# Head 0's preparation rebuilt: whole-row loads joined on SBUF, four reads of its turned tile, operands copied on SBUF

## The chip, the cores and the metric

The kernel runs on one core of one Trainium2 chip. The metric is the device time of one execution in microseconds, the median of several runs. TensorE, VectorE, ScalarE, GpSimd and SyncE (SP) each work through their own instructions strictly in order; DMAs are issued from SP's and GpSimd's queues.

## The reference, cut to what matters

Three stages follow one another. The first is attention with a bucket mask (2 batches, 8 heads, 768 positions, 64 channels); its output, 1536 tokens by 512, goes through two feed-forward stages.

```python
q_bits = (einsum('bhsd,dk->bhsk', q, proj) > 0);  k_bits = (einsum('bhsd,dk->bhsk', k, proj) > 0)   # 6 bits
mask   = q_bucket[:, :, :, None] == k_bucket[:, :, None, :]        # the bits as a number, 0 to 63
scores = where(mask, q @ k.T / sqrt(64), -1e9)
attn   = exp(scores - max) / (sum + 1e-9);   x = attn @ v          # then heads side by side
h = x @ w_in;  g = h * tanh(softplus(h));    x = g @ w_out         # d_ff 2048
out = ((x @ w1) * (x @ w2)) @ w3 @ w_out2                          # d_ff 1024
```

## The kernel before

The 16 heads (two batches of eight) are worked off one after another; head u has six row blocks of 128 queries. Each block has one score tile S of 128 x 768 in two PSUM banks (two halves of 384 columns), a maximum on VectorE (L619), an exponential on ScalarE (L622), six transposes of it (L666) and products with v (L695). Numbers are split into a rounded part and a remainder so that matmuls in a rounded format keep single precision: a score is the sum of two matmuls per half, one of the operands `kb`, `qb` (128 rows: rounded part and remainder of k and q) and one of `ka`, `qa` (76 rows: the rounded parts again, and 12 rows of mask).

`prep` (L485) makes these four operands for a head. `load_head` (L448) puts q and k of the head into one tile `rw`, so that each 128-position block holds q's 64 channels beside k's 64; every DMA piece is therefore 256 bytes. Six TensorE transposes (L514) turn it: PSUM tile with q's channels on partitions 0 to 63 and k's on 64 to 127. For heads 1 to 15 ScalarE writes the rounded part `hh` (L532) and VectorE the remainder (L534), each for all 128 partitions, and six DMAs (`move`, L480) put their halves where `qb`, `kb`, `qa`, `ka` want them; bucket bits come from matmuls with `psel2` on `hh` and the remainder (L565). For head 0 that way is not used: twelve reads of the turned tile of 64 x 384 each, six on ScalarE (L547) and six on VectorE (L550 to L557), write the operands directly, and the bits come from four matmuls per half on `qb` and `kb` with another selector, `psel`. A comparison (L576) then writes the mask rows into `qa`, and a copy (L443 for head 0, a DMA for the others) takes twelve of them to `ka`.

The turned tile and the bits tile lie, for head 0 and for heads from 3 on, in one two-bank score tile (`self.one`); heads 1 and 2 use two separate one-bank tiles. `HH` has two buffers, one head's `hh` and remainder; before, head 0 doesn't use it.

The order of all this isn't written by hand. `Plan.op` takes each step with its engine, an expected cost, an expected latency (`lat`), its reads and writes, and a due number; `Plan.run` is a list scheduler that gives every engine its order by these, and every engine's queue then holds that order. `after` only puts a step behind another's planned start. Between planned TensorE steps up to 60 us the plan fills gaps with zero matmuls (`zeros`, L427) that keep the engine running. At the start, `setup` (L1213) prepares constants: GpSimd sets tiles to zero, VectorE splits the projection into `pq` and fills `psel`, GpSimd fills `psel2` from `pq`. Behind it in GpSimd's queue stand sums over v (L465) and then the first weight loads (L754).

Of the kernel before, what the change touches and what calls it, by code (L numbers as in the profile page):

```python
# [320 lines left out]
def kernel(  # L321
# [14 lines left out]
    nc = tc.nc  # L336
# [73 lines left out]
    psel = ctile([128, 2, 2, 128], "psel", FR)  # L410
# [11 lines left out]
    v_id, v_psel, v_psel2, v_ccol, v_qks = Val(), Val(), Val(), Val(), Val()  # L422
# [25 lines left out]
    def load_head(u, due, after=()):  # L448
        b, h = divmod(u, H)
        t = raws[u] = Val(RW, "r")  # L450
        for x, (nm, src) in enumerate((("q", q), ("k", k))):
            P.op("SP", 0.5, lambda x=x, src=src: nc.sync.dma_start(
                out=t()[:, :, x], in_=src[b, h].rearrange("(p c) d -> p c d", c=C)), w=[(t, nm)], due=due,
                lat=None if u else 1.85, name=f"load{nm}{u}", after=after)

    def load_v(u, due, after=()):
        b, h = divmod(u, H)
        t = vs[u] = Val(VP, "v")
        P.op("SP", 0.5, lambda: nc.sync.dma_start(out=t(), in_=v[b, h].rearrange("(p c) d -> p c d", c=C)),
# [18 lines left out]
    def move(o, to, f, fr, r, w, due, name):  # L478

        P.op("SP", 0.5, lambda: nc.sync.dma_start(out=o()[to].bitcast(F32), in_=f()[fr].bitcast(F32)),  # L480
             r=r, w=w, due=due, lat=5.0, name=name)
# [3 lines left out]
    def prep(u, d0, step):  # L485
# [30 lines left out]
        hh, ll = (Val(HH, "h"), Val(HH, "l")) if u else (None, None)  # L516
        if u and t.one:
            P.op("PE", C * 0.118, tr, r=[raw], w=t.all() + [(hh, "t"), (ll, "t")], due=d(1), name=f"tq{u}", after=first_bits)
        else:
            for a in range(2):  # L520
                P.op("PE", CH * 0.118, lambda t=t, a=a: tr(t, range(a * CH, (a + 1) * CH)), r=[raw],
                     w=[t.key(a)] + ([(hh, "t"), (ll, "t")] if u and not a else []), due=d(1), name=f"tq{u}", after=first_bits if u else ())
        low, high = slice(0, D), slice(D, 2 * D)
        half = lambda v_: v_.rearrange("p (a n) -> p a n", a=2)
        if u:
            for x in ((slice(0, 2), ) if t.one else (slice(0, 1), slice(1, 2))):
                n = (x.stop - x.start) * HS
                cols = slice(x.start * HS, x.stop * HS)
                key = t.all()[x]
                src = (lambda t=t: t.v[0]()[:, :, 0:HS]) if t.one else (lambda t=t, x=x: t.at(x.start))  # L530
                dst = (lambda v_: half(v_())) if t.one else (lambda v_, cols=cols: v_()[:, cols])
                P.op("ACT", act(n) + 0.01, lambda src=src, dst=dst: nc.scalar.activation(  # L532
                    out=dst(hh), in_=src(), func=AF.Copy, scale=qks[:, 0:1]), r=key + [v_qks], w=[(hh, x.start)], due=d(1.3), name=f"hh{u}")
                P.op("DVE", dve(n), lambda src=src, dst=dst: nc.vector.scalar_tensor_tensor(  # L534
                    out=dst(ll), in0=src(), scalar=qks[:, 0:1], in1=dst(hh), op0=ALU.mult, op1=ALU.subtract),
                    r=key + [(hh, x.start), v_qks], w=[(ll, x.start)], due=d(1.6), name=f"ll{u}")
            for o, to, f, fr in ((qb, low, hh, low), (kb, high, hh, high), (qa, low, hh, low), (ka, low, hh, high),
                                 (qb, high, ll, low), (kb, low, ll, high)):
                move(o, to, f, fr, [f], [(o, to.start if o in (qb, kb) else "x")], d(2.2), f"fa{u}")
            ops = [(psel2[:, 0], hh), (psel2[:, 1], hh), (psel2[:, 0], ll)]  # L540
            needs = [hh, ll, v_psel2]
        else:
            inv = 1.0 / float(D) ** 0.5
            for a in range(2):
                cols = slice(a * HS, (a + 1) * HS)
                for o, p, fr, c in ((kb, high, high, inv), (ka, low, high, inv), (qb, low, low, 1.0)):
                    P.op("ACT", act(HS), lambda t=t, o=o, p=p, fr=fr, c=c, a=a, cols=cols: nc.scalar.activation(  # L547
                        out=o()[p, cols], in_=t.at(a)[fr], func=AF.Copy, scale=c), r=[t.key(a)],
                        w=[(o, ("x" if o is ka else p.start, a))], due=d(1.3 + 0.3 * a), name=f"hh{u}")
                P.op("DVE", dve(HS), lambda t=t, a=a, cols=cols: nc.vector.tensor_copy(out=qa()[low, cols], in_=t.at(a)[low]),  # L550
                     r=[t.key(a)], w=[(qa, ("x", a))], due=d(1.3 + 0.3 * a), name=f"hh{u}")
                P.op("DVE", dve(HS), lambda t=t, a=a, cols=cols: nc.vector.tensor_sub(
                    out=qb()[high, cols], in0=t.at(a)[low], in1=qa()[low, cols]), r=[t.key(a), (qa, ("x", a))],
                    w=[(qb, (D, a))], due=d(1.4 + 0.3 * a), name=f"ll{u}")
                P.op("DVE", dve(HS), lambda t=t, a=a, cols=cols: nc.vector.scalar_tensor_tensor(
                    out=kb()[low, cols], in0=t.at(a)[high], scalar=inv, in1=kb()[high, cols],
                    op0=ALU.mult, op1=ALU.subtract), r=[t.key(a), (kb, (D, a))], w=[(kb, (0, a))], due=d(1.5 + 0.3 * a), name=f"ll{u}")  # L557
            ops = [(psel[:, 0, 0], qb), (psel[:, 1, 0], kb), (psel[:, 0, 1], qb), (psel[:, 1, 1], kb)]
            needs = [qb, kb, v_psel]
# [7 lines left out]
        for a in range(2):  # L567
            r = needs if u else [(qb, (x, a)) for x in (0, D)] + [(kb, (x, a)) for x in (0, D)] + [v_psel]
# [18 lines left out]
        for a in range(2):  # L587
# [3 lines left out]
                 r=[(qa, ("m", a))], w=[(ka, ("m", a))], due=d(4.6), name=f"km{u}")  # L591

# [34 lines left out]
    def norm(u, due):  # L627
# [25 lines left out]
        P.op("SP", 0.5, lambda: nc.sync.dma_start(  # L653
# [161 lines left out]
    def wprod(f, d0, d1):  # L815
# [40 lines left out]
        P.op("SP", 0.5, lambda: nc.sync.dma_start(out=wp_d[f * 128:(f + 1) * 128], in_=o()[:, 0:DM]), r=[o], w=[(v_wp, f)],  # L856
# [9 lines left out]
    def x_split(n, due, after=()):  # L866
# [3 lines left out]
        for kk in range(KD):  # L870
# [5 lines left out]
            for e in range(2):  # L876
                P.op("SP", 0.5, lambda e=e, kk=kk, rb=rb: nc.sync.dma_start(
# [62 lines left out]
    def x_quarters(due, after=()):  # L940
        xs = []
        for i in range(2):
            xq_ = Quarters()
            xs.append(xq_)
            for n in (1, 2):
                t0, t1 = n * TB, (n + 1) * TB
                bs = range(t0 // S, (t1 - 1) // S + 1)
                for k1 in range(2):
# [5 lines left out]
                    for e in range(2):  # L954
                        P.op("SP", 0.5, lambda e=e, kk=kk, rb=rb, t0=t0, t1=t1: nc.sync.dma_start(
# [114 lines left out]
    def ff_first(n, d0, d1):  # L1070
# [107 lines left out]
        def o_group(G):  # L1178
# [3 lines left out]
            for t4 in range(TB // 128):  # L1182
# [15 lines left out]
                if G == GT // 2 - 1:  # L1198
                    P.op("SP", 0.5, lambda t4=t4, ov=ov: nc.sync.dma_start(out=rows_out(n, t4), in_=ov()), r=[(oacc, t4)],
                         due=dd(1.0), lat=3.0, name="out")  # L1200
# [12 lines left out]
    def setup():  # L1213
        pr = Val()
        for e in range(2):
            P.op("SP", 0.5, lambda e=e: nc.sync.dma_start(out=prow[e * D:(e + 1) * D], in_=proj), w=[(pr, e)], due=-10, lat=2.2, name="proj")
        cr, pz, p2z = Val(F4, "c"), Val(), Val()
# [9 lines left out]
        P.op("POOL", 0.5, lambda: nc.gpsimd.memset(psel.bitcast(F32), 0.0), w=[pz], due=-11, name="pz")  # L1227
        P.op("POOL", 0.8, crows, w=[cr], due=-10, name="crow")
        P.op("POOL", 0.2, lambda: nc.gpsimd.memset(psel2.bitcast(F32), 0.0), w=[p2z], due=-9, name="p2z")
# [18 lines left out]
        def pqs():  # L1248
            nc.vector.tensor_copy(out=pq[:, 0, 0], in_=prow)
# [293 lines left out]
```

## Time and profile before

| | |
|---|---|
| median of 3 runs | 781.59 us (781.08 to 782.19) |
| profiled execution | 781.81 us, its span 780.0 us |
| TensorE matmul / weight load | 765.0 us (98%) / 596.7 us (76%) of the span |
| VectorE / ScalarE / GpSimd | 557.8 us (72%) / 508.9 us (65%) / 105.4 us (14%) |
| DMA | 120.70 MB, of it 55.02 MB through SP's queue and 65.02 MB through GpSimd's |

Busy shares are means over the span. The chain that ended last is TensorE's for 91% of the span, with short pieces of VectorE (4%), ScalarE (2%) and DMA (1%); a matmul's end is modelled, so a TensorE shown busy is not one at its peak. A row's "idle before <- X" says how long the engine stood and what released it.

### The profile page before, as it was taken

The page shows a single profiled execution, that of the slowest core. Times are in us where ns is not written, and L with a number is a line of the kernel's source. Part 1 is how long each engine was busy: PE and PEld are TensorE (multiplying, and loading weights), DVE is VectorE, ACT ScalarE, POOL GpSimd, SP SyncE. Part 2 cuts the span into 40 slices and gives each one's busy share as a digit, 9 for nine tenths or more (in the row PEclk, how much of TensorE's full clock was granted, in tenths as well). Part 3 has the DMA queues.
Part 4 walks back from the last instruction along what each step waited for, and adds up shares of the span by engine and source line. Part 5 has one row for each costly group of instructions (what it writes and reads, how often), then busy time and mean ns, then how long its engine had stood idle before and what let it go on. Part 6 is the DMA issues. An engine that isn't in the chain of part 4 may idle for free.

```text
span 780.0 us, 10577 instructions
## 1 busy us (share of the span) xinstructions
PE 765.0 (98%) x3808; PEld 596.7 (76%) x3808; DVE 557.8 (72%) x812; ACT 508.9 (65%) x815; POOL 105.4 (14%) x204
## 2 busy tenths in 40 slices
PE   6999999999999999999999999999999999999998
PEld 5767888897577777777766888888888888788877
DVE  3897778889877986967996959764543848775620
ACT  3889667779799887868867835654544626443330
POOL 3222001222332222113212110000000000000000
PEclk8999999999999999999999999999999999999999
DMA  6997646697897768755465740431215310010011
GB/s 206 214 305 229 181 128 200 157 336 218 259 280 220 249 207 255 230 175 165 158 230 203 259 147 28 162 103 39 75 54 162 109 54 1 28 54 1 1 54 55
DMA packets 62252, 120.70 MB, mean 155 GB/s; under 512 B 29924, under 2 KB 32324, under 8 KB 61176
## 3 DMA queue, kind: packets, MB, share of 16 engines
q1 hardware_dynamic: 45944, 55.02, 25.4%
q0 software_dynamic: 16256, 65.02, 24.2%
q8 instruction: 30, 0.49, 0.3%
q14 instruction: 22, 0.18, 0.1%
HBM read 83.89 MB, written 17.87 MB: 130 GB/s over the span
## 4 chain that ended last, share of the span: by engine, by line
PE 91%; DVE 4%; ACT 2%; issue 1%; DMA 1%; SPq 0%; ACTq 0%; DVEq 0%
PE q L1005 20%; PE b L1419 11%; PE b L1065 9%; PE s L606 8%; PE b L695 8%; PE b L666 7%; PE b L1160 6%; PE b L1049 5%; PE b L846 5%; PE b L1461 5%; PE s L565 2%; PE s L514 1%; PE b L829 1%; DVE st L619 1%; DMA ka<-qa 1%
## 5 line engine op out<-in xcount | busy, mean ns | idle before, releaser
L1005 PE MATMUL q<-k,k 128*128 128x512 f32 x672 | 159.4, 395 | 0.0
L1005 PEld LDWEIGHTS q<-k,k 128*128 128x128 f32 x672 | 126.1, 188 | 30.4 <-DVE f L1020 0.4
L798 DVE TENSOR_TENSOR k<-f,k 128x1024 fp32r<-128x1024 f32 x92 | 111.7, 1220 | 20.5 <-ACT k L796 20.2
L796 ACT CAST k<-f 128x1024 fp32r<-128x1024 f32 x92 | 94.7, 1050 | 21.0 <-DVE f L988 6.4
L619 DVE TENSOR_REDUCE st<-s 128x1 f32<-128x768 f32 x96 | 90.9, 950 | 21.7 <-PE s L606 19.4
L622 ACT ACTIVATE E<-s,st 128x768 f32<-128x768 f32 x96 | 86.9, 905 | 25.1 <-DVE st L619 15.2
L666 PE MATMUL b<-ident,E 128*128 128x128 f32 x576 | 92.0, 274 | 0.2 <-DVE T L675 0.2
L1016 ACT COPY f<-q 128x512 f32<-128x512 f32 x64 | 37.5, 586 | 81.6 <-PE q L1005 78.6
L1020 DVE TENSOR_TENSOR f<-q,f 128x512 f32<-128x512 f32 x64 | 42.9, 686 | 65.8 <-PE q L1005 39.5
L1419 PE MATMUL b<-k,k 128*128 128x512 f32 x384 | 89.6, 393 | 0.0
L666 PEld LDWEIGHTS b<-ident,E 128*128 128x128 f32 x576 | 71.4, 140 | 23.7 <-issue 7.2
L1419 PEld LDWEIGHTS b<-k,k 128*128 128x128 f32 x384 | 72.1, 188 | 16.6
L1065 PE MATMUL b<-k,k 128*128 128x512 f32 x288 | 78.2, 404 | 0.0
L1065 PEld LDWEIGHTS b<-k,k 128*128 128x128 f32 x288 | 51.5, 188 | 15.2 <-issue 6.0
L695 PE MATMUL b<-T,v 128*64 128x384 f32 x288 | 62.4, 511 | 0.0
L606 PE MATMUL s<-kb,qb 128*128 128x384 f32 x192 | 56.7, 376 | 1.4 <-ACT E L622 1.1
L1049 PE MATMUL b<-k,k 128*128 128x512 f32 x192 | 54.5, 407 | 0.0
L443 ACT COPY T<-b 128x384 f32<-128x384 f32 x94 | 43.9, 483 | 15.2 <-PE b L666 13.8
L846 PE MATMUL b<-k,k 128*128 128x512 f32 x192 | 52.1, 405 | 0.0
L606 PE MATMUL s<-ka,qa 76*128 76x384 f32 x192 | 49.9, 341 | 0.6 <-DMA ka<-qa 0.6
L1160 PE MATMUL b<-k,k 128*128 128x512 f32 x192 | 47.4, 396 | 0.0
L1461 PE MATMUL b<-k,f 128*128 128x512 f32 (+1 forms) x216 | 46.4, 370 | 0.8 <-ACT f L1451 0.5
(143 smaller groups left out, 1117.7 us busy)
## 6 DMA issues: line engine op xcount, KB each, us to landing
k<-in_moe_w_dram POOLq DMA_DIRECT2D x16, 1024.0 KB, 5.9
k<-in_moe_w_out_dram POOLq DMA_DIRECT2D x12, 1024.0 KB, 7.8
k<-in_moe_w_in_dram POOLq DMA_DIRECT2D x8, 1024.0 KB, 8.0
f<-keep_wo SPq DMA_DIRECT2D x16, 512.0 KB
qb<-hh SPq DMA_DIRECT2D x30, 192.0 KB
kb<-hh SPq DMA_DIRECT2D x30, 192.0 KB
keep_wi<-f POOLq DMA_DIRECT2D x8, 512.0 KB, 7.0
f<-keep_wi POOLq DMA_DIRECT2D x8, 512.0 KB, 7.0
```

The source lines that it names most:

```text
L606: nc.tensor.matmul(t()[:, a, 0:HS], lhsT=l()[0:kk, i * 128:(i + 1) * 128], rhs=r()[0:kk, a * HS:(a + 1) * HS], start=(l is qb), stop=(l is ...
L619: P.op("DVE", 0.868, lambda: nc.vector.tensor_reduce(out=s()[:, 0, i:i + 1], in_=t()[:, :, 0:HS], axis=AX.XY, op=ALU.max, negate=True), r= ...
L666: nc.tensor.transpose(t()[:, ci * 128:(ci + 1) * 128], es[ci]()[:, kt * 128:(kt + 1) * 128], ident)
L695: nc.tensor.matmul(t()[r, 0:HS], lhsT=w, rhs=f(), start=first and j == 0, stop=last and j == CH - 1)
L796: P.op("ACT", act(1024, True), lambda: nc.scalar.copy(out=hl()[:, 0:1024], in_=f()), r=[f], w=[(hl, 0)], due=due, name="hi")
L798: vec(0, 1024, lambda v_: v_.tensor_sub(out=hl()[:, 1024:2048], in0=f(), in1=hl()[:, 0:1024]), r=[f, (hl, 0)], w=[(hl, 1)], due=due + 0.1, ...
L846: nc.tensor.matmul(acc(), lhsT=hv()[:, ws, g_, :], rhs=wview(wo2[g_ // 2], 2)[:, rs, g_ % 2, :], start=(n == 0), stop=(n == 3 * GT - 1))
L1005: nc.tensor.matmul(qs[q](), lhsT=lhs(w, i), rhs=xs[i].at(xs[i].hl[x], o), start=first and n == 0, stop=n == 5, skip_group_check=True)
L1049: nc.tensor.matmul(of(), lhsT=wview(w, KD)[:, ws, kk, (f % 2) * 128:(f % 2) * 128 + 128], rhs=kview(xhl[n][kk // 2], xs, kk), start=(m == ...
L1065: nc.tensor.matmul(of(), lhsT=l(), rhs=rr(), start=(m == 0), stop=(m == len(ops) - 1))
L1160: nc.tensor.matmul(t(), lhsT=wview(w, KD)[:, ws, kk, f2 * 128:f2 * 128 + 128], rhs=kview(x2[kk // 2], xs, kk), start=(kk == 0 and s == 0), ...
L1419: nc.tensor.matmul(t(), lhsT=wview(w, 2)[:, ws, f, dd * 128:(dd + 1) * 128], rhs=gv[:, gs, f, :], start=(j == 0 and f == 0 and s == 0), st ...
```

## The change

Only head 0's way through `load_head` and `prep`, the constants that it needs, and the planned cost of SP's DMAs are changed.

- `load_head(0)`: q and k land in two halves of an `F4` buffer, each partition's 1536 bytes in one piece; two VectorE copies of 128 x 384 join them into `rw`.
- `prep(0)`: head 0 takes the way of the other heads: per half one ScalarE read (`hh`) and one VectorE read (remainder) of the turned tile, into the two `HH` buffers. The planner is given these reads so that ScalarE may be on half 1 while VectorE is on half 0. Four of the six operand copies are then SBUF copies for head 0 (two on ScalarE, two on VectorE, 64 x 768 each); `qa` and `ka` are filled by DMA.
- bits: three matmuls per half with `psel2`; `psel` is gone, and the projection is split on GpSimd.
- `first_bits` also holds head 0's last mask copy, so the plan starts head 1's transposes behind its planned start.
- every SP DMA planned at 0.5 is planned at 0.65; two planned latencies for head 0 are new (1.5 for a load, 2.0 for an operand copy), and the planned cost of the `hh` read is 0.15 above its formula, not 0.01 (0 for head 0 before).

```diff
 def load_head(u, due, after=()):
+        f = None if u else Val(F4, "c")
         for x, (nm, src) in enumerate((("q", q), ("k", k))):
-            P.op("SP", 0.5, lambda x=x, src=src: nc.sync.dma_start(
+            if u == 0:
+                row = lambda x=x: f()[:, x * C * D:(x + 1) * C * D].rearrange("p (c d) -> p c d", c=C)
+                P.op("SP", 0.65, lambda row=row, src=src: nc.sync.dma_start(
+                    out=row(), in_=src[b, h].rearrange("(p c) d -> p c d", c=C)), w=[(f, nm)], due=due, lat=1.5, name=f"load{nm}{u}")
+                P.op("DVE", dve2(C * D), lambda x=x, row=row: nc.vector.tensor_copy(out=t()[:, :, x], in_=row()), r=[(f, nm)],
+                     w=[(t, nm)], due=due, name=f"join{u}")
+                continue
+            P.op("SP", 0.65, lambda x=x, src=src: nc.sync.dma_start(
...
 def prep(u, d0, step):
-        hh, ll = (Val(HH, "h"), Val(HH, "l")) if u else (None, None)
-        if u and t.one:
+        hh, ll = Val(HH, "h"), Val(HH, "l")
+        halves = not (u and t.one)
+        if not halves:
...
-            for a in range(2):
-                cols = slice(a * HS, (a + 1) * HS)
-                for o, p, fr, c in ((kb, high, high, inv), (ka, low, high, inv), (qb, low, low, 1.0)):
-                    P.op("ACT", act(HS), lambda t=t, o=o, p=p, fr=fr, c=c, a=a, cols=cols: nc.scalar.activation(
-                        out=o()[p, cols], in_=t.at(a)[fr], func=AF.Copy, scale=c), r=[t.key(a)], ...)
-                P.op("DVE", dve(HS), lambda ...: nc.vector.tensor_copy(out=qa()[low, cols], in_=t.at(a)[low]), ...)
-                P.op("DVE", dve(HS), lambda ...: nc.vector.tensor_sub(
-                    out=qb()[high, cols], in0=t.at(a)[low], in1=qa()[low, cols]), ...)
-                P.op("DVE", dve(HS), lambda ...: nc.vector.scalar_tensor_tensor(
-                    out=kb()[low, cols], in0=t.at(a)[high], scalar=inv, in1=kb()[high, cols], ...), ...)
-            ops = [(psel[:, 0, 0], qb), (psel[:, 1, 0], kb), (psel[:, 0, 1], qb), (psel[:, 1, 1], kb)]
+        for x in (slice(0, 1), slice(1, 2)) if halves else (slice(0, 2), ):
+            P.op("ACT", act(n) + 0.15, lambda src=src, dst=dst: nc.scalar.activation(
+                out=dst(hh), in_=src(), func=AF.Copy, scale=qks[:, 0:1]), r=key + [v_qks], w=[(hh, x.start)], ...)
+            P.op("DVE", dve(n), lambda src=src, dst=dst: nc.vector.scalar_tensor_tensor(
+                out=dst(ll), in0=src(), scalar=qks[:, 0:1], in1=dst(hh), op0=ALU.mult, op1=ALU.subtract), ...)
+        for o, to, f, fr, e in ((qb, low, hh, low, "ACT"), (kb, high, hh, high, "ACT"), (qa, low, hh, low, ""), (ka, low, hh, high, ""),
+                                (qb, high, ll, low, "DVE"), (kb, low, ll, high, "DVE")):
+            if u or not e:
+                move(o, to, f, fr, [f], w, d(2.2), f"fa{u}", None if u else 2.0)
+            else:
+                P.op(e, act(S, True) if e == "ACT" else dve2(S), lambda ...: copy(e, o()[to], f()[fr]), r=[f], w=w, ...)
+        ops = [(psel2[:, 0], hh), (psel2[:, 1], hh), (psel2[:, 0], ll)]
...
+        first_bits.append(P.units[-1])
...
 def setup():
-        P.op("POOL", 0.5, lambda: nc.gpsimd.memset(psel.bitcast(F32), 0.0), w=[pz], due=-11, name="pz")
-            nc.vector.tensor_copy(out=pq[:, 0, 0], in_=prow)          # and two more, and four into psel
-        P.op("DVE", 0.7, pqs, r=[pr, pz], w=[v_psel], due=-9, name="pqs")
+            nc.gpsimd.tensor_copy(out=pq[:, 0, 0], in_=prow)          # and two more, and four into psel2
+        P.op("POOL", 1.4, pqs, r=[pr, p2z], w=[v_psel2], due=-9, name="pqs")
```

## Rows read from the trace of the kernel before

**Rows 1.** The page's first part: busy time, share of the span, instructions.
```profile
PE 765.0 (98%) x3808; PEld 596.7 (76%) x3808; DVE 557.8 (72%) x812; ACT 508.9 (65%) x815; POOL 105.4 (14%) x204
```

**Rows 2.** Three stretches: length, then each engine's busy time, clock, DMA share, GB/s.
```profile
0.00:18.00 18.00, 10.59 (x36) 8.57 (x37) 6.16 (x17) 6.55 (x12) 6.76 (x28) 0.83 0.64 194
30.00:60.00 30.00, 29.29 (x179) 19.17 (x176) 28.55 (x41) 27.14 (x53) 8.65 (x14) 1.00 0.97 290
60.00:775.00 715.00, 711.71 (x3516) 557.37 (x3516) 513.39 (x743) 466.25 (x732) 89.10 (x159) 1.00 0.47 148
```

**Rows 3.** Chain of waits up to 18 us: start, length, what.
```profile
0.73 0.69 SPq L452
1.48 3.54 DMA rw<-in_k_dram
5.15 1.53 PE s L514 x6
...
8.79 0.49 ACT kb L547
...
9.31 0.56 DVE qb L552
...
9.90 0.49 ACT ka L547
...
12.70 0.56 DVE qb L552
...
13.40 1.62 PE s L565 x4
```

**Rows 4.** Timeline, 15 to 19 us: start, length, engine, line, tiles.
```profile
15.06 1.29 DVE L576 TENSOR_SCALAR qa<-s,ccol 64x384 fp32r<-64x384 f32 x2 [1.80 <-PE s L565]
...
17.00 0.51 ACT L443 CAST ka<-qa 12x384 fp32r<-12x384 f32 x1
17.01 0.62 DVE L534 SCALAR_TENSOR_TENSOR hh<-b,qks,hh 128x384 fp32r<-128x384 f32 x1 [0.67 <-ACT hh L532]
...
17.54 0.58 ACT L532 ACTIVATE hh<-b,qks 128x384 fp32r<-128x384 f32 x1
...
18.02 0.77 PE L606 MATMUL s<-ka,qa 76*128 76x384 f32 x2
...
18.83 0.96 DVE L619 TENSOR_REDUCE st<-s 128x1 f32<-128x768 f32 x1
```

**Rows 5.** Stretches by what the DMA engines moved (columns as in rows 2).
```profile
2.25:4.00 1.75, 1.22 (x3) 0.64 (x3) 0.16 (x1) 0.07 (x1) 0.47 (x4) 1.00 0.92 207
5.25:5.75 0.50, 0.50 (x3) 0.50 (x4) 0.00 (x0) 0.00 (x0) 0.00 (x0) 1.00 0.97 334
11.00:13.50 2.50, 1.05 (x5) 0.78 (x5) 1.66 (x3) 0.49 (x1) 2.16 (x4) 0.65 0.03 13
13.50:26.00 12.50, 12.50 (x63) 11.85 (x64) 8.09 (x11) 6.92 (x15) 0.00 (x0) 0.80 1.01 294
```

**Rows 6.** Groups by line and form: count, busy us, mean ns, idle before.
```profile
L796 ACT CAST k<-f 128x1024 fp32r<-128x1024 f32 x92 | 94.7, 1050 | 21.0 <-DVE f L988 6.4 <-PE b L1419 5.3 <-PE b L1065 4.3
...
L443 DVE CAST f<-v 128x384 fp32r<-128x384 f32 x1 | 0.3, 348 | 0.0
```

**Rows 7.** Timeline, 8 to 29 us.
```profile
8.12 0.77 POOL L1264 CAST psel<-pq 64x12 fp32r<-64x12 f32 x4 [5.29 <-DVE pq L1250]
...
11.63 0.88 POOL L754 DMA_DIRECT2D k<-in_moe_w_out_dram  x1
...
26.74 0.62 DVE L534 SCALAR_TENSOR_TENSOR hh<-b,qks,hh 128x384 fp32r<-128x384 f32 x1 [0.41 <-DMA kb<-hh]
...
28.32 0.59 PE L606 MATMUL s<-kb,qb 128*128 128x384 f32 x2
```

**Rows 8.** The chain at 207 us; the list of TensorE's waits, whole run.
```profile
207.36 6.78 DMA ka<-qa
...
PE s L606 <- DMA ka<-qa: 0.6, 1, 0.6
```

More of the change, by code (lines that the diff above doesn't have):

```diff
@@ L458, in load_v @@
         t = vs[u] = Val(VP, "v")
[L459 removed]
+        P.op("SP", 0.65, lambda: nc.sync.dma_start(out=t(), in_=v[b, h].rearrange("(p c) d -> p c d", c=C)),
              w=[t], due=due, name=f"loadv{u}", after=after)
@@ L521, in prep @@
                 P.op("PE", CH * 0.118, lambda t=t, a=a: tr(t, range(a * CH, (a + 1) * CH)), r=[raw],
-                     w=[t.key(a)] + ([(hh, "t"), (ll, "t")] if u and not a else []), due=d(1), name=f"tq{u}", after=first_bits if u else ())
+                     w=[t.key(a)] + ([] if a else [(hh, "t"), (ll, "t")]), due=d(1), name=f"tq{u}", after=first_bits if u else ())
         low, high = slice(0, D), slice(D, 2 * D)
         half = lambda v_: v_.rearrange("p (a n) -> p a n", a=2)
[L525 to L543, printed above, removed]
-            for a in range(2):
-                cols = slice(a * HS, (a + 1) * HS)
-                for o, p, fr, c in ((kb, high, high, inv), (ka, low, high, inv), (qb, low, low, 1.0)):
-                    P.op("ACT", act(HS), lambda t=t, o=o, p=p, fr=fr, c=c, a=a, cols=cols: nc.scalar.activation(
[L548 to L557, printed above, removed]
-            ops = [(psel[:, 0, 0], qb), (psel[:, 1, 0], kb), (psel[:, 0, 1], qb), (psel[:, 1, 1], kb)]
-            needs = [qb, kb, v_psel]
@@ new lines, in prep @@
+        for x in (slice(0, 1), slice(1, 2)) if halves else (slice(0, 2), ):
+            n = (x.stop - x.start) * HS
+            cols = slice(x.start * HS, x.stop * HS)
+            key = t.all()[x]
+            src = (lambda t=t, x=x: t.at(x.start)) if halves else (lambda t=t: t.v[0]()[:, :, 0:HS])
+            dst = (lambda v_, cols=cols: v_()[:, cols]) if halves else (lambda v_: half(v_()))
+            P.op("ACT", act(n) + 0.15, lambda src=src, dst=dst: nc.scalar.activation(
+                out=dst(hh), in_=src(), func=AF.Copy, scale=qks[:, 0:1]), r=key + [v_qks], w=[(hh, x.start)],
+                due=d(1.3 + 0.1 * x.start), name=f"hh{u}")
+            P.op("DVE", dve(n), lambda src=src, dst=dst: nc.vector.scalar_tensor_tensor(
+                out=dst(ll), in0=src(), scalar=qks[:, 0:1], in1=dst(hh), op0=ALU.mult, op1=ALU.subtract),
+                r=key + [(hh, x.start), v_qks], w=[(ll, x.start)], due=d(1.4 + 0.1 * x.start), name=f"ll{u}")
@@ new lines, in prep @@
+        for o, to, f, fr, e in ((qb, low, hh, low, "ACT"), (kb, high, hh, high, "ACT"), (qa, low, hh, low, ""), (ka, low, hh, high, ""),
+                                (qb, high, ll, low, "DVE"), (kb, low, ll, high, "DVE")):
+            w = [(o, to.start if o in (qb, kb) else "x")]
+            if u or not e:
+                move(o, to, f, fr, [f], w, d(2.2), f"fa{u}", None if u else 2.0)
+            else:
+                P.op(e, act(S, True) if e == "ACT" else dve2(S), lambda o=o, to=to, f=f, fr=fr, e=e: copy(e, o()[to], f()[fr]), r=[f], w=w,
+                     due=d(2.2), name=f"fa{u}")
@@ L567, in prep @@
         for a in range(2):
-            r = needs if u else [(qb, (x, a)) for x in (0, D)] + [(kb, (x, a)) for x in (0, D)] + [v_psel]
+            r = ([(hh, a), (ll, a)] if halves else [hh, ll]) + [v_psel2]
             P.op("PE", pe(HS, len(ops)), lambda a=a: bits(a), r=r, w=[t.key(a)], due=d(4), name=f"bits{u}")
@@ L1248, in pqs @@
         def pqs():
-            nc.vector.tensor_copy(out=pq[:, 0, 0], in_=prow)
-            nc.vector.tensor_sub(out=pq[:, 0, 1], in0=prow, in1=pq[:, 0, 0])
-            nc.vector.tensor_scalar(out=pq[:, 1], in0=pq[:, 0], scalar1=-1.0, scalar2=None, op0=ALU.mult)
-            for j in range(2):
-                for g in range(2):
-                    o = D + 32 * j + NB * g
-                    nc.vector.tensor_copy(out=psel[:, j, :, o:o + NB], in_=pq[:, (j + g) % 2])
-        P.op("DVE", 0.7, pqs, r=[pr, pz], w=[v_psel], due=-9, name="pqs")
-        def p2():
+            nc.gpsimd.tensor_copy(out=pq[:, 0, 0], in_=prow)
+            nc.gpsimd.tensor_sub(out=pq[:, 0, 1], in0=prow, in1=pq[:, 0, 0])
+            nc.gpsimd.tensor_scalar(out=pq[:, 1], in0=pq[:, 0], scalar1=-1.0, scalar2=None, op0=ALU.mult)
             for j in range(2):
```

32 lines of the change are left out of this document (15 added, 17 removed).

## The prediction

> **What bounds the kernel now.** The page comes first: TensorE is busy for 98% of the span, in two thirds of it beside busy VectorE and ScalarE [rows 1]. The table by stretches shows where it is not [rows 2]. From 60 to 775 us TensorE is idle for 3.3 us in all (715.00 less 711.71); in 30 to 60 the narrow engines are VectorE and ScalarE, at 28.55 and 27.14 of 30 us. In 0 to 18 TensorE works only 10.59 us, on head 0's preparation and zero matmuls. So nearly everything after the first score tile is a full pipe, and time is to be had before it. The chain of waits tells what fills those 18 us [rows 3]: q's load is issued in 0.69 us, k's takes 3.54 us from issue, six transposes 1.53, then twelve reads of one PSUM tile, strictly one after another from 6.68 to 13.26, then head 0's second half of bucket bits for 1.62. A look at the order within those reads matters: VectorE's read at 9.31 is of half 0 and follows ScalarE's read of half 1 (8.79); ScalarE's next one (9.90, half 1) follows VectorE's. The two halves lie in two banks of one tile, and still one engine waits for the other. Then come the comparison, the copy of the mask rows, and the first complete scores at 18.02; their maximum starts at 18.83 [rows 4].
>
> **The change part by part**, on the profiled run's clock (span 780.0, the execution 781.81 us, 1.81 around the span; the runs' median is 781.59, 0.22 less, and the sum is taken off that, 781.6).
>
> *Load and join.* q and k are 393 KB. In pieces of 256 bytes the DMA engines moved 207 GB/s at a share of 0.92; in the window in which v's whole rows begin, 334 GB/s at 0.97 [rows 5]. 393 KB take 1.90 us at the one and 1.18 at the other: the landing comes 0.72 us sooner, at 4.30 in place of 5.02. The least is nothing, if the 3.54 us are latency throughout. The second join is a new step on the path: VectorE's one copy of 128x384 from SBUF took 348 ns [rows 6]. Transposes then start at about 4.80 (0.35 sooner); bounds 4.4 and 5.5.
>
> *Reads of the turned tile.* Twelve become four: two ScalarE reads of 128x384 with a scale and two VectorE subtractions. Head 1 has the same pairs at 0.58 and 0.62 us [rows 4], there in two separate tiles, where the ScalarE read at 17.54 starts before VectorE's ends. Head 0 keeps one tile with two banks. By rows 3 that means all four in a row, whatever the banks: 2 x 0.58 + 2 x 0.62 + three gaps of 0.02 = 2.46 us, where there were 6.58. Transposes end at 6.33, ScalarE's reads at 7.53, VectorE's at 8.80. The Trainium skill, page "PSUM — Partial Sum Buffer", section "PSUM bank collisions raise a hardware error", says that two engines collide only in one bank and on the same partitions, and that different banks run clean. By that rule the second ScalarE read and the first subtraction would overlap, 0.6 us less; rows 3 show this kernel waiting across banks, so the measurement decides, and the rule is a rival below.
>
> *Bits.* Three matmuls each half in place of four: 1.62 x 3/4 = 1.2 us, at the half clock of 13.4 to 15.0; the granted clock was 0.65 over 11 to 13.5 [rows 5], and a TensorE with less waiting may keep more. With the 0.14 us issue gap the bits end at 10.14. Their weights now come from GpSimd alone. Its four small casts took 0.77 us behind a 5.29 us wait for VectorE [rows 7]; seven such steps make 1.35 us, and until 7.5 there is room even if they start at 6. If that cover went, each us later is a us on the path.
>
> *Operand copies.* Four copies of 64x768 on SBUF replace eight of the old reads. ScalarE's: 1.05 us for 1024 columns bounds each [rows 6], so both end by 9.6, beside the subtractions. VectorE's: the 348 ns of 384 columns, and twice that, bound each; I take the middle, 0.52. They end at 9.86, still ahead of the bits, and the comparisons behind them in VectorE's queue lose nothing. The two copies left to DMA start at 7.5; at 0.65 us an issue, the second is issued at 8.2 and lands at 11.7, if it takes what k's load took. The worst in the trace is 6.78 us [rows 8], that is 15.
>
> *Comparison, mask, scores.* The two comparisons take 1.29 us, the second mask copy 0.51 [rows 4]: 10.18, 11.47, 12.0. The first full score matmul follows at 12.3 in place of 18.02: 5.7 us. Head 1's two ScalarE reads now stand behind this mask copy (they were before it), and its subtractions may stand ahead of the first maximum on VectorE: that starts between 12.9 and 13.8, not at 18.83, so 5.0 to 5.9 sooner. I take 5.5.
>
> *Head 1.* Its working tiles are now shared with head 0, so its reads wait for head 0's two DMA copies (about 11.7, hidden). Its six copies stay on DMA, and the DMA engines were at a share of 1.01 from 13.5 to 26 [rows 5]: 2 MB of weights, head 3's q and k, head 1's copies. This block shifts only as far as the weights' issue, which stands in GpSimd's queue behind the v sums at 11.63 [rows 7]; GpSimd gets there 0 to 2.5 us sooner, I take 1.3. VectorE's wait at 26.74 shows the last copy landing there [rows 7], so then 25.4. Head 1's scores began at 28.32; moved by 5.5 they would begin at 22.8, before their operands. The price is 0 (the planner reckons with 5 us for a copy and fills the time with other work) to 2.6 us; I take 1.0, since heads 0 and 1 share queues that cannot pass a waiting instruction.
>
> *Planned SP cost 0.5 to 0.65.* This costs nothing itself; it may reorder any queue. The trace's load took 0.69 us to issue [rows 3], so the plan comes nearer to it. Value 0, bounds -1.6 (half of TensorE's idle time after 60) and +6.
>
> Sum: 781.6 - 5.5 + 1.0 = 777.1.
>
> **The rivals.** *A, the forecast*, 777.1, its own range 775.9 to 778.3; chance 42%.
> *B, DMA backlog gives back more*: the whole 2.6 us is lost at head 1. For it: a share of 1.01, and in-order queues. Against: ScalarE and VectorE have decoding work waiting there. 781.6 - 5.5 + 2.6 = 778.7; 17%.
> *C, the banks are read at once and nothing is given back*: 781.6 - 5.5 - 0.6 = 775.5; for it, the overlap in head 1 with two tiles; against, rows 3; 18%. (This is what the skill's bank rule would give; no row here shows it for one tile.)
> *D, slower*: with the new issue costs the mask rows of later heads (a DMA behind loads and six copies on SP) come late. In the trace this happens once: 6.78 us from issue, and TensorE idle for it for 0.6 us [rows 8]. At 0.6 us per head in 10 of the 14 later heads it is 6.0 us: 781.6 - 4.5 + 6.0 = 783.1. It decides from 0.32 us a head on. Against it: once in fifteen such copies is the whole of it before, and the plan's issue costs come nearer to the trace; 13%.
> *E, the change doesn't do what it says in the time*: reordered work between 30 and 220, where VectorE and ScalarE are nearly full, takes back what the start gives: 781.6 - 4.5 + 4.3 = 781.4; 10%.
>
> **How the numbers follow.** Faster takes in A, B and C: 0.77; no change is E, 0.10; slower is D, 0.13; 0.2% of 781.6 is 1.6 us, about what can be told from none. The range goes from 774.0 (C with the early bound of the load and a kept clock) to 782.6, half of D, leaving out about a tenth on each side.
>
> **What would show it.** Transposes at 4.8, not 5.15; four reads of the turned tile and no two of them overlapping; bits ending near 10; the first scores with the mask at 12.3 and the first maximum near 13.3; head 1's first scores between 22.8 and 25.4, the latter behind a DMA copy. From 60 us on each landmark should stand 4 to 5 us earlier than before, and the last matmul too. The forecast is wrong if the first scores come later than 14, if the landmarks' lead shrinks between 30 and 220, or if TensorE's idle time after 60 us grows past 3.3 us by more than the start gave.

## The result, and the profile after

The changed kernel takes 788.49 us (median of 4, 786.92 to 789.47) beside 781.47 for the kernel before: ratio 1.0086, interval 1.0074 to 1.0098. It is slower by 7 us; 777.1 was forecast, and the range ended at 782.6. The profiled execution took 788.75 us, its span 787.0. Line numbers below are those of each kernel's own file.

The page's first part hardly moves [rows 1]:
```profile
PE 767.1 (97%) x3808; PEld 595.9 (76%) x3808; DVE 559.6 (71%) x810; ACT 508.2 (65%) x808; POOL 98.7 (13%) x206
```
The three stretches [rows 2] say more. The first holds 13.74 us of TensorE's work instead of 10.59, at full clock. From 60 on TensorE is idle for 7.66 us (715.00 less 707.34); it was 3.29.
```profile
0.00:18.00 18.00, 13.74 (x64) 11.41 (x65) 10.16 (x17) 8.52 (x15) 7.17 (x30) 1.00 0.83 239
30.00:60.00 30.00, 28.68 (x174) 19.08 (x173) 28.29 (x39) 25.64 (x50) 8.03 (x14) 0.99 0.86 270
60.00:775.00 715.00, 707.34 (x3469) 551.72 (x3468) 515.91 (x748) 465.16 (x727) 82.79 (x159) 1.00 0.47 148
```
The chain of waits up to 13 us [rows 3] shows the start as the change wants it: k lands at 3.73, the turned tile is read in four steps from 5.81 to 8.12, and the first maximum starts at 12.49, where it was 18.83 [rows 4].
```profile
1.18 2.55 DMA f<-in_k_dram
...
3.75 0.37 DVE rw L456
...
4.16 1.55 PE s L521 x6
...
5.81 1.06 ACT hh L539 x2
...
6.96 1.16 DVE hh L542 x2
...
8.71 0.98 DVE kb L442
...
11.88 0.59 PE s L601 x2
...
12.49 0.06 DVE st L614
```
The timeline from 13 to 27 us shows the first loss. SP's issue of head 1's first operand copy (line 487) takes 2.09 us, where its neighbours take 0.6; ScalarE and VectorE wait over 3 us for head 1's copies to land before they can take up head 2, and TensorE 3.40 us for head 1's scores:
```profile
13.39 2.09 SPq L487 DMA_DIRECT2D qb<-hh  x1
...
24.42 0.58 ACT L539 ACTIVATE hh<-b,qks 128x384 fp32r<-128x384 f32 x1 [3.28 <-DMA ka<-hh]
26.14 0.62 DVE L542 SCALAR_TENSOR_TENSOR hh<-b,qks,hh 128x384 fp32r<-128x384 f32 x1 [3.81 <-DMA kb<-hh]
26.27 0.59 PE L601 MATMUL s<-kb,qb 128*128 128x384 f32 x2 [3.40 <-DMA kb<-hh]
```
The second loss is far behind the change. A pair of loads from r_d (a buffer in DRAM through which the reciprocals of the rows' sums go), issued by SP at 218.13, holds VectorE up at 225.85; ScalarE waits for VectorE, TensorE for ScalarE (timeline):
```profile
208.99 5.64 SPq L466 DMA_DIRECT2D v<-in_v_dram  x1
...
218.13 1.18 SPq L872 DMA_DIRECT2D f<-r_d  x2
...
225.85 0.69 DVE L878 TENSOR_TENSOR f<-k,f 128x512 f32<-128x512 f32 x1 [3.68 <-DMA f<-r_d]
...
229.57 0.62 ACT L890 CAST k<-f 128x512 fp32r<-128x512 f32 x1 [5.04 <-DVE f L888]
...
230.24 0.50 PE L1044 MATMUL b<-k,k 128*128 128x512 f32 x1 [3.18 <-ACT k L890]
```
In the kernel before, the same pair, the fourth of its kind, is issued ten us earlier (timeline):
```profile
208.26 1.85 SPq L877 DMA_DIRECT2D f<-r_d  x2
...
216.68 0.69 DVE L883 TENSOR_TENSOR f<-k,f 128x512 f32<-128x512 f32 x1 [0.89 <-DMA f<-r_d]
```
From its issue to VectorE's read it takes about 8 us in both kernels. What differs is its place in SP's list: the kernel before has it ahead of a head's q and k loads, the changed kernel behind such loads, a load of v whose issue alone takes 5.64 us, and three operand copies. This is read from the two traces; no run moved the pair alone.

In stretches of 4 us (columns as in rows 2) TensorE works 1.53 of 4 us there, and the next 4 us run at a mean granted clock of 0.58, so mostly at the lower level, 1.2 GHz: the stall is paid twice.
```profile
228.00:232.00 4.00, 1.53 (x5) 1.05 (x6) 3.28 (x4) 1.83 (x3) 1.05 (x2) 0.99 1.00 373
232.00:236.00 4.00, 4.00 (x19) 3.29 (x19) 1.81 (x3) 3.58 (x5) 0.00 (x0) 0.58 1.03 395
```
Each head has six maxima on VectorE. The start of a head's first one, in us, for the kernels that matter below (e3 to e11 are runs of the next two sections; each column is the one profiled execution of its kernel):
```
head    before   after      e3      e5      e7     e11
0        18.83   12.49   13.47   13.08   13.01   13.39
1        29.30   27.32   28.70   23.79   26.04   23.86
2        48.59   50.16   48.01   43.05   45.82   43.24
9       214.84  214.98  213.75  209.14  212.95  209.36
10      241.41  248.74  240.81  236.02  239.24  236.03
last    410.74  418.32  410.13  405.35  408.57  405.37
```
After: 6.3 us ahead at head 0, 2.0 at head 1, nothing left by head 2; level at head 9, 7.3 behind at head 10, and so to the end. Where two kernels differ in their order, a single maximum is a loose mark (the changed kernel is 4.8 behind at head 8 and level at head 9); e3 to e11 keep one order and can be compared head by head.

### The profile page after: what moved, and what is told of

The parts are those of the page before. It is cut to its first block, busy times and chain, and to the rows that moved or that the text cites. A ratio compares the mean times of both kernels' runs of the same rounds, so it can differ in the third digit from the quotient of the medians.

```text
span 787.0 us, 10576 instructions
## 1 busy us (share of the span) xinstructions
PE 767.1 (97%) x3808; PEld 595.9 (76%) x3808; DVE 559.6 (71%) x810; ACT 508.2 (65%) x808; POOL 98.7 (13%) x206
## 4 chain that ended last, share of the span: by engine, by line
PE 85%; DVE 9%; DMA 2%; issue 2%; ACT 1%; SPq 0%; DVEq 0%; ACTq 0%
PE q L1000 20%; PE b L1405 11%; PE b L1060 9%; PE b L690 7%; PE s L601 7%; PE b L661 6%; PE b L1155 6%; PE b L841 5%; PE b L1044 5%; PE b L1447 5%; DVE st L614 2%; PE s L521 1%; PE s L559 1%; DVE qa L570 1%; DMA f<-r_d 1%
## 5 line engine op out<-in xcount | busy, mean ns | idle before, releaser
L661 PE MATMUL b<-ident,E 128*128 128x128 f32 x576 | 93.7, 277 | 0.2 <-DVE T L670 0.2
L601 PEld LDWEIGHTS s<-kb,qb 128*128 128x128 f32 x192 | 30.0, 190 | 27.8 <-issue 12.8
L442 ACT COPY T<-b 128x384 f32<-128x384 f32 x87 | 40.3, 478 | 13.6 <-PE b L661 12.8
```

The source lines that it names most:

```text
L601: nc.tensor.matmul(t()[:, a, 0:HS], lhsT=l()[0:kk, i * 128:(i + 1) * 128], rhs=r()[0:kk, a * HS:(a + 1) * HS], start=(l is qb), stop=(l is ...
L661: nc.tensor.transpose(t()[:, ci * 128:(ci + 1) * 128], es[ci]()[:, kt * 128:(kt + 1) * 128], ident)
```

## The experiments: is it the order?

All instructions are put in order by a list scheduler from planned costs, so a change of any cost can move any instruction of any engine. The planner also picks the engine of the steps that either ScalarE or VectorE can do; in what follows, "order" means its whole plan. First theory (P): the new planned SP cost did it. Rivals: H, the new start itself; S, any touch of the input scatters the order.

**e1**, the kernel before with SP's planned cost changed, in all places:
```diff
-        P.op("SP", 0.5, lambda: nc.sync.dma_start(
+        P.op("SP", 0.65, lambda: nc.sync.dma_start(
```


> The kernel before, with one planned cost changed in all of the program: the time that the order's planner books for a DMA issue on SP, 0.5 to 0.65 us. No instruction is added or removed; only their order on the engines can change. Theory P (the loss after 30 us is the re-planned order, and this cost is what re-planned it): 786 to 790, with a stall of 5 us or more somewhere behind 30 us that the kernel before has not, and the start as before (first scores at 18.0). Rival H (the loss comes from head 1's operands and what follows from the new start, not from the order): 781 to 782.5. Rival S (any change of any planned cost scatters the order by several us, this one no more than another): between 779 and 790, to be read beside the control with the ACT cost.


784.82 us, ratio 1.0031 (1.0018 to 1.0044): 2.7 us slower than the kernel before in the same runs (782.08), with the same work, less than P wanted. Five of the steps that either engine can do went from ScalarE to VectorE (the page counts 810 and 817 instructions, it was 815 and 812). The list of TensorE's waits from 200 to 250 us has a wait for a mask row, the kind of rival D on record:
```profile
PE s L606 <- DMA ka<-qa: 2.2, 1, 2.2
```

**e2**, the changed kernel with that cost back:
```diff
-        P.op("SP", 0.65, lambda: nc.sync.dma_start(
+        P.op("SP", 0.5, lambda: nc.sync.dma_start(
```


> The changed kernel with the planned cost of a DMA issue on SP back at 0.5 us; everything else of the change stays. Theory P (SP's planned cost alone): the stall at 218 to 231 us goes, 780 to 782 (the start's 6 us, less 5 lost at head 1). Rival H: 788, as the changed kernel. Rival S: the order is planned anew all the same, by head 0's new instructions; 780 to 788, the stall in another place or none.


787.80 us, 1.0075 (1.0060 to 1.0090). P falls.

**e3**, the changed kernel with the scheduler's choice replaced by a written list: its own up to head 0's first scores, then that of the kernel before:
```diff
+        for name, n, e, s, *zero in json.loads(zlib.decompress(base64.b64decode(ORDER))):
...
+            u = by.pop((name, n))
...
+            u.fn(e) if len(u.alts) > 1 else u.fn()
```


> The changed kernel's instructions, in its own order up to head 0's first scores, and from there in the order of the kernel before on every engine (written out, not planned). Theory P and rival S (re-planned order loses about 7 us behind 30 us): 779.5 to 782, first scores at 11.9, no stall of 3 us at 218 to 231, head 1's first scores still at about 26.3 since the weights' transfers are unchanged. Rival H (the loss follows from the new start itself): 786 to 789. The forecast on record, were head 1's price 1 us and the order free: 777.


781.43 us, 1.0003 (0.9990 to 1.0016). The order is worth 7.1 us (788.49 less 781.43; 6.5 by the two ratios, since the two were run beside the kernel before at different times). So H falls as an account of the slowdown. In the list, e3 has five VectorE steps less than the changed kernel and five ScalarE steps more; what the engines chosen are worth apart from the order is not separated. The stall at 218 to 231 is gone, and the lead stays at 0.6 from head 1 to head 10 (table). The start's gain is gone all the same, between head 0 and head 1.

**e4**, control, the kernel before with the planned cost of the hh read changed as in the change:
```diff
-                P.op("ACT", act(n) + 0.01, lambda src=src, dst=dst: nc.scalar.activation(
+                P.op("ACT", act(n) + 0.15, lambda src=src, dst=dst: nc.scalar.activation(
```


> Control: the kernel before, with another planned cost changed, that of ACT's copy of q and k out of the turned tile (hh, from 0.01 to 0.15 us over its base, as the change books it). Instructions unchanged. Theory P and rival H: 781 to 782.5, as the kernel before. Rival S (any touch of a planned cost scatters the order): 3 us or more from the kernel before, to either side, 785 the likeliest.


788.32 us, 1.0078 (1.0063 to 1.0094): as slow as the changed kernel with none of its new instructions. The table by stretches has the largest part of its loss in the same place; from 180 to 260 us TensorE worked 77.56 us in the kernel before, 2.9 us more than here:
```profile
180.00:260.00 80.00, 74.67 (x405) 52.26 (x404) 63.78 (x94) 68.69 (x117) 19.99 (x38) 1.00 0.82 243
```
It is not the same stall, though: in e4 the fourth r_d pair is issued at 210.30, and TensorE's waits from 216 to 250 us are short ones, the longest 1.4 us, for ScalarE. Before 180 us it loses another 1.8 us.

That left open whether this number is the cause (N) or any number will do (S). Four runs tell. **e13**: the changed kernel with both costs back for the later heads (SP's by e2's edit). **e14**: with that of hh alone. **e15** and **e16**: the kernel before with costs that the change leaves alone.
```diff
-            P.op("ACT", act(n) + 0.15, lambda src=src, dst=dst: nc.scalar.activation(
+            P.op("ACT", act(n) + (0.01 if u else 0.15), lambda src=src, dst=dst: nc.scalar.activation(
...
-        P.op("POOL", 0.9, sc, r=[s], w=[(s, 2)], due=due, name=f"norm{u}")
+        P.op("POOL", 0.95, sc, r=[s], w=[(s, 2)], due=due, name=f"norm{u}")
...
-        P.op("DVE", 0.868, lambda: nc.vector.tensor_reduce(
+        P.op("DVE", 0.878, lambda: nc.vector.tensor_reduce(
```


> The changed kernel with both planned costs that reach every head as they were before: SP's DMA issue 0.5, ScalarE's copy hh of the later heads 0.01 over its base. Head 0's new instructions and their costs stay. Theory N (the ScalarE number re-planned the order for the worse): 780.5 to 782, like the new start in the old order. Theory S (head 0's new instructions alone are touch enough): 783.5 to 788.

> The changed kernel with ScalarE's planned cost alone taken back (SP's stays at 0.65). Theory N: 780.5 to 784, the upper end if SP's 0.65 costs its 2.7 us here too. Theory S: 784 to 789.

> The kernel before with a planned cost that the change does not touch: GpSimd's step per head, 0.90 to 0.95. Instructions unchanged. Theory N: 781.3 to 782.3, as the kernel before. Theory S: 783.5 to 788.

> The kernel before with another one that the change does not touch: VectorE's maximum of a score tile, 0.868 to 0.878, which is nearer to what it takes (0.95). Instructions unchanged. Theory N: 781.3 to 782.3. Theory S: 783.5 to 788.


e13 785.11 (1.0047, 1.0029 to 1.0064); e14 785.60 (1.0045, 1.0021 to 1.0068); e15 784.28 (1.0032, 1.0021 to 1.0043); e16 788.34 (1.0090, 1.0066 to 1.0115). They are 2.6 to 6.7 us slower than the kernel before in the same runs, as S has it (e16 lies just above its range). Four of four touches of one cost made the kernel before slower (e1, e4, e15, e16), and all four plans made for the new start (the changed kernel, e2, e13, e14) are 3.7 to 7.1 us slower than e3. So the order of the kernel before is the best of nine tried, and a planned cost moved by 0.01 us loses it (e16).

Three limits. N is not wholly gone: with the cost of hh back, the changed kernel is 2.9 us faster (e14 against 788.49), while SP's alone gives back 0.7, within the noise (e2). e13 does not isolate head 0's new instructions either: the change also moves the due number of the remainder's read for every later head from 1.6 to 1.4, which its list of parts does not name, and e13 keeps that. And the losses have a place in common, though not one stall: from head 7 to head 10 the changed kernel, e2, e4 and e16 fall back by 5.0 to 5.5 us against the kernel before, e1 by 3.4, e14 by 2.2, e15 by 0.7, e13 not at all.

## The experiments: where the start's gain goes

From here on all kernels with the new start have e3's written order, so that each edit stands alone. In e3 ScalarE stands 4 us before head 2's first read of the turned tile, waiting for the buffer that head 1's last copy still reads; the copy T behind it comes late, and TensorE waits 3.42 us (timeline). Then the clock is low: two matmuls of 128x384 take 0.99 us instead of 0.59. Last, stretches:
```profile
24.05 0.58 ACT L750 ACTIVATE hh<-b,qks 128x384 fp32r<-128x384 f32 x1 [4.01 <-DMA ka<-hh]
...
25.05 0.87 PE L901 MATMUL b<-T,v 128*64 128x384 f32 x4 [3.42 <-ACT T L653]
...
25.75 0.62 DVE L753 SCALAR_TENSOR_TENSOR hh<-b,qks,hh 128x384 fp32r<-128x384 f32 x1 [4.74 <-DMA kb<-hh]
...
27.04 0.99 PE L812 MATMUL s<-kb,qb 128*128 128x384 f32 x2
```
```profile
24.00:28.00 4.00, 2.95 (x13) 2.29 (x14) 2.25 (x4) 3.43 (x7) 0.28 (x1) 0.72 0.67 113
28.00:32.00 4.00, 4.00 (x24) 2.31 (x22) 3.48 (x6) 3.65 (x11) 1.49 (x4) 0.85 0.95 217
```
The DMA view of 12 to 18.7 us (queue, packets, MB, share) shows what the copies met. q0 carries GpSimd's weights, q1 all of SP's transfers:
```profile
q0 software_dynamic: 533, 2.05, 80.2%
q1 hardware_dynamic: 1105, 0.31, 19.6%
```
SP's queue moves 0.31 MB in 6.7 us beside 2.05 MB of weights, in packets of some 0.28 KB against 3.8. The Trainium skill, page "DMA: Bandwidth & Descriptors", section "Queues, rings and completion order", says that an engine takes turns between its queues, a packet at a time. The trace agrees as far as both queues move on together and the queue of the larger pieces gets most of the bytes; it shows no turns of one for one, since q1 moved twice as many of the profile's packets as q0.

Theory Q: this backlog takes the lead. Rivals: R, what follows 30 us takes it back whatever head 1 does; B, head 1 waits for buffers or SP and not for the transfers.

**e5** and **e6**: the first two weight transfers are replaced by zeros (new start; kernel before, whose own order is written out as a list too):
```diff
-        P.op("POOL", 1.0, lambda: nc.gpsimd.dma_start(
+        P.op("POOL", 1.0, (lambda: nc.gpsimd.memset(raw().bitcast(F32), 0.0)) if nm in ("w20", "w21") else lambda: nc.gpsimd.dma_start(
```


> The new start with the old order (781.4 us) and the first two weight transfers of 1 MB (issued by GpSimd at 10.0 and 11.0 us) left out: GpSimd writes zeros to their tiles instead, so the values of two weight blocks are wrong. Theory Q (the start's 5 us are lost at 26 to 30 us because head 1's copies stand behind these transfers on the DMA engines): head 1's first scores at 20 to 22 instead of 27, the lead at 30 us 4 to 5.5, the time 776 to 777.5. Rival R (what follows takes the lead back whatever head 1 does, because the stretch 30 to 60 us is bound by ACT, DVE or later transfers): head 1 early, but 780 to 781.5 at the end. Rival B (head 1 waits for its buffers or for SP, not for the transfers): head 1's scores at 25 or later, 780.5 to 781.5.

> The kernel before with the same two transfers left out and zeros written in their place. It says what of the last run's gain is the start's. Theory Q: head 1's copies land earlier here too, but its head 0 is ready only at 18.0 and PE is busy from 18 to 28 with it; its first scores move from 28.3 by 1 at most, 780.5 to 782. Rival R: as the kernel before, 781.5 to 782.3. If it gains 4 us or more, the transfers were a brake of their own and the start is worth nothing even with them gone.


e5 778.75 (0.9952, 0.9934 to 0.9970), e6 781.69 (1.0000, 0.9991 to 1.0009). The transfers cost the kernel before nothing and the new start 2.7 us at the median, 4.8 between the profiled executions (780.99 and 776.22): half of its gain or more. The median misses Q's range of 776 to 777.5. Of e5's five executions two took 776.2 to 776.3, the profiled one among them, and three 778.8 to 779.7; what parts them is not shown. In the profiled one the lead is 5.75 at head 0 and 5.4 at head 10: what follows takes hardly anything back, and R falls. B falls too: with the same buffers and the same list on SP, head 1's scores come 4.5 us earlier than in e3. Head 2's read and head 1's scores (22.55, where Q had 20 to 22) come at:
```profile
20.06 0.58 ACT L750 ACTIVATE hh<-b,qks 128x384 fp32r<-128x384 f32 x1 [0.57 <-DMA ka<-hh]
...
22.55 0.59 PE L812 MATMUL s<-kb,qb 128*128 128x384 f32 x2
```

**e7**, nothing left out: head 1's four copies made on SBUF too:
```diff
-            if u or not e:
+            if u > 1 or not e:
```


> The new start with the old order, and head 1's four operand copies made on SBUF by ACT (two) and DVE (two), as the change does for head 0; only qa and ka still go by DMA. Nothing is left out. Theory Q: four transfers of some 0.85 us less ahead of head 1's last one: first scores of head 1 at 23 to 24 instead of 27, ACT's hh of head 2 at 20 to 21 instead of 24.05, 777.5 to 779.5. Rival R: 780.5 to 782. Rival B: 780.5 to 782. DVE is full from 12 to 18 us (5.5 of 6 busy), so its two copies (1.4 us) may delay head 0's maxima by as much; then 779 to 780.5 under Q.


779.25 us, 0.9966 (0.9952 to 0.9980): faster than e3 and than the kernel before, and in Q's range. Head 1's scores at 24.63 (late by 0.6 against Q); the next wait in line is again for a DMA:
```profile
23.66 0.62 DVE L753 SCALAR_TENSOR_TENSOR hh<-b,qks,hh 128x384 fp32r<-128x384 f32 x1 [2.05 <-DMA ka<-hh]
24.63 0.60 PE L812 MATMUL s<-kb,qb 128*128 128x384 f32 x2
```

**e8** (e3) and **e9** (e7) put two issues of SP's list later, the loads of head 3's q and k behind head 1's transfers (fa1 in the scheduler's names; the lines show e8's list, unpacked; in e9 fa1[2] and fa1[3] alone are left on SP):
```diff
-loadq3 loadk3 fa1[0] fa1[1] fa1[2] fa1[3] fa1[4] fa1[5]
+fa1[0] fa1[1] fa1[2] fa1[3] fa1[4] fa1[5] loadq3 loadk3
```


> The new start with the old order, but the loads of head 3's q and k rows, which SP issues at 11.75 and 12.39 us ahead of head 1's copies, stand behind them on SP. Theory Q: their 1.9 us on the DMA engines (from the weights' landing at 18.7 to 20.7) go out of head 1's way; head 1's first scores at 25 to 25.5 instead of 27, 779.5 to 780.5. Rivals R and B: 781 to 782.

> Head 1's four copies on SBUF (779.25 us) and head 3's row loads behind head 1's two remaining transfers on SP. Theory Q: with the copies off the queue, the rows' 1.9 us are the next thing ahead of qa and ka; VectorE's subtraction of head 2, which waited 2.05 us for ka at 23.66, starts at 21.8, head 1's first scores 1 to 2 us earlier, 777 to 778.5. Rival (ACT and DVE are the bound by now, with the extra copies): 778.8 to 779.6. The move by itself, with the copies still transferred, was worth 0.3 us.


e8 781.10 (0.9991, 0.9981 to 1.0001): not to be told from e3, and head 1's first maximum stands at 28.61 against 28.70. Q's number for it was wrong: with six copies behind the weights, two loads less change little; why is not shown. e9 778.03 (0.9949, 0.9935 to 0.9964): in Q's range, though the interval touches e7's. VectorE's wait of 2.05 us is gone; that read starts at 22.21. Head 1's scores start at 24.15, only 0.5 us earlier, not 1 to 2.

**e10**, e7 with head 0's turned tile as two tiles of one bank:
```diff
-                self.one = not 0 < u <= CFG["tb"]
+                self.one = not first and not 0 < u <= CFG["tb"]
...
-        t = Halves()
+        t = Halves(u == 0)
```


> Head 1's four copies on SBUF (779.25 us), and head 0's turned tile is two PSUM tiles of one bank each instead of one of two banks. In the changed kernel VectorE's first subtraction (6.96) starts only when both of ScalarE's reads are done (6.86), and it alone carries a wait on ScalarE. Theory W (it is the wait that the tile brings, not the bank): the first subtraction starts at 6.4, right behind ScalarE's first read and beside its second, both engines reading PSUM at once at unchanged durations (0.58 and 0.62); VectorE ends at 7.65 instead of 8.10, the first scores 0.3 to 0.5 earlier. Rival P (PSUM itself keeps the engines apart): starts at 6.9 as before, or the reads grow to 0.8 or more. Of the end time, where head 1 is the bound: 778.8 to 779.5 either way.


Theory W holds for the reads (timeline):
```profile
5.10 1.16 ACT L750 ACTIVATE hh<-b,qks 128x384 fp32r<-128x384 f32 x2 [2.79 <-PE b L732]
5.71 1.19 DVE L753 SCALAR_TENSOR_TENSOR hh<-b,qks,hh 128x384 fp32r<-128x384 f32 x2 [1.60 <-ACT hh L750]
```
VectorE starts when ScalarE's first read ends; the pairs take 1.16 and 1.19 us against 1.06 and 1.16 one after the other in the changed kernel. Two banks are read at once at nearly full speed; the Trainium skill's rule cited on record (page "PSUM — Partial Sum Buffer", section "PSUM bank collisions raise a hardware error") fits this row. In the changed kernel it was the wait on the one tile that kept them apart. The time, 778.68 (0.9954, 0.9937 to 0.9970), cannot be told from e7's, and the first maximum comes 0.26 later, not earlier: TensorE now waits 1.9 us for the next head's rows (0.8 in e7), which DMA brings no sooner (list of waits, 11 to 40 us):
```profile
PE b L732 <- DMA rw<-in_k_dram: 1.9, 1, 1.9
```

**e11**, e9 with head 1's two copies of the remainder (ll in the code) on GpSimd instead of VectorE and the two weight issues behind them; **e12**, the same with two tiles:
```diff
+            if u == 1 and e == "DVE":
+                e = "POOL"
             if u > 1 or not e:
...
-        (nc.scalar.copy if e == "ACT" else nc.vector.tensor_copy)(out=o, in_=i)
+        (nc.scalar.copy if e == "ACT" else nc.gpsimd.tensor_copy if e == "POOL" else nc.vector.tensor_copy)(out=o, in_=i)
```


> The new start and old order; head 1's hh copies by ScalarE, its ll copies by GpSimd, and behind these on GpSimd's queue the two weight transfers (issued after 14.5 instead of 10); head 3's rows behind head 1's qa and ka. Nothing is left out. Theory Q: head 1's qa and ka land by 16 to 18, first scores of head 1 at 20 to 22 as with the weights left out; GpSimd's copies, not seen in any row so far, are free if under 2 us each. Head 2's copies at 22 to 27 meet the weights' end instead; ScalarE's first decode of a weight stands at 28.5 less the lead of 5, so a landing after 24 costs the difference. 776 to 778.5. Rival (the weights moved collide with head 2's transfers and the decode, and the lead is lost there): 779.5 to 782.

> The last one, with head 0's turned tile as two tiles of one bank. Theory W: 0.3 to 0.5 us less than without, 775.5 to 778. Rival P: as without.


e11: 776.73 us, 0.9944 (0.9928 to 0.9961), the lowest median of those that leave nothing out, in Q's range. Its interval overlaps e9's, since one of its ten executions took 782.77; eight of the ten lie below every execution of e9. It changes two things against e9, and which of them counts is not shown. GpSimd's copies take 0.82 us each, the weights are issued at 15.04, head 1's scores start at 22.89 (20 to 22 expected), and in the profiled execution the lead is 5.44 at heads 0 and 1 alike, 5.4 at head 10:
```profile
13.38 0.82 POOL L653 CAST qb<-hh 64x768 fp32r<-64x768 f32 x1 [3.23 <-DVE hh L753]
...
15.04 1.67 POOL L962 DMA_DIRECT2D k<-in_moe_w_out_dram  x2
...
22.89 0.59 PE L814 MATMUL s<-kb,qb 128*128 128x384 f32 x2
```
e12: 777.96 (0.9948, 0.9933 to 0.9963). Two tiles again give nothing at the end: W's 0.3 to 0.5 us did not come.

## Why the prediction was wrong

- *Load and join.* Right in kind. k landed at 3.73 instead of 4.30, and the transposes began at 4.16, below the bound of 4.4: whole rows saved 0.99 us from issue to landing, not 0.72.
- *Reads.* Right: four in a row, 2.3 us (2.46 on record), and for the reason given, a wait that spans the banks of one tile. Rival C's overlap came only with two tiles (e10).
- *Bits and copies.* TensorE kept full clock to 18 us, where half was taken, and the bits were done by 8.6 instead of 10.14. Then VectorE's last copy held the scores up: it took 0.97 us, not 0.52. GpSimd's sums over v ran beside it (timeline of the changed kernel):
```profile
8.14 0.56 DVE L442 CAST qb<-hh 64x768 fp32r<-64x768 f32 x1
8.68 0.59 POOL L472 TENSOR_TENSOR vs<-v 128x192 f32<-128x192 f32 x1 [1.28 <-DMA v<-in_v_dram]
8.71 0.97 DVE L442 CAST kb<-hh 64x768 fp32r<-64x768 f32 x1
9.34 0.52 POOL L473 TENSOR_TENSOR vs<-vs 128x64 f32<-128x64 f32 x1
```
  The runs bear this out: such a copy took 0.55 to 0.56 us wherever GpSimd was idle (eight copies in e7, e9, e10 and e12) and 0.85 to 0.97 wherever two of these sums ran beside it (nine kernels). In e7, where the copy started just before the sum, it took 0.56 and the sum 1.00 instead of 0.59. No run moved the sums on purpose.
- *First maximum.* 12.49, 6.3 us sooner; 5.5 was taken, with 5.9 as the bound.
- **Head 1: failed.** "I take 1.0" of at most 2.6. In e3, with the order of before, the lead falls from 5.35 at head 0 to 0.60 at head 1: the price is 4.75, and e5, without the weights, keeps 5.5 of 5.75 at head 1. The transfer block was seen [rows 5] and its landing well placed (25.4 on record; head 2's subtraction was let go at 25.75 in e3). What was not priced: head 2 needs the buffers that head 1's copies read, so ScalarE and VectorE queue behind the landing too, and the decoding work on which the odds against rival B rested stands behind them (in e3 it starts at 28.51); and after 3.4 us of idleness TensorE's clock is low. Rival B named the mechanism, at half its price.
- **Planned SP cost: failed.** That a new plan "may reorder any queue" was said and then valued at 0, with bounds of -1.6 and +6. The order as a whole costs 6.5 to 7.1 us, above the upper bound, and this cost alone does not make it: with SP's back at 0.5 the kernel still takes 787.80 (e2), though on the kernel before it costs 2.7 (e1). The planned cost of hh, which the change raises for every head, has no term in the prediction at all; alone it costs the kernel before 6.2 us (e4).
- *The rivals.* E named reordered work, at 4.3 us and between 30 and 220; the longest stall lies at 218 to 231. D forecast a slower kernel, but by waits for mask rows; such waits are there in e1, e14 and e16 and not in the changed kernel's list of TensorE's waits. Its direction came out, its mechanism did not.
- The sum with what was measured: 781.6 - 5.4 (the lead in e3 at head 0) + 4.8 (head 1) + 7.1 (order) = 788.1, beside 788.49. It had to close nearly, since the last term is the difference of two of these times; what it shows is how the parts divide.

Open: why a changed cost makes just these orders, whether the r_d pair moved forward alone would end the stall at 218 to 231 us, and whether a planned order as good as the old one exists for the new start. None was tried.

## What to carry to other kernels

Where a scheduler orders everything from planned costs, first measure how far the time scatters when a cost that doesn't matter is touched; a gain smaller than that is only seen with the order held fixed. A gain at the start is kept only if the next stage's inputs come earlier by as much: look at what occupies the DMA engines just then, and move what isn't needed yet behind it. Price a wait for a DMA by everything queued behind the waiting instruction, buffers of the next stage and TensorE's clock afterwards among it.

## What the runs showed of the hardware

- Two queues on the same DMA engines do not share bytes evenly: 2.05 MB against 0.31 MB in 6.7 us (e3), and one issue on SP then took 2.10 us instead of 0.6.
- GpSimd copied 64x768 on SBUF in 0.82 us, as fast as ScalarE (0.83); VectorE took 0.55 alone, and up to 0.97 beside GpSimd's sums over v.
- Two engines read two PSUM banks at once with little loss (e10: 1.16 and 1.19 us for the pairs, 1.06 and 1.16 in turn); with both banks in one tile they took turns (changed kernel).
- TensorE's granted clock was low in the stretch after a stall of 3 us: 0.58 behind the one at 230 us in the changed kernel, 0.72 and 0.85 around and behind the one that ends at 25 us in e3.
